# Output product in seven block products instead of eight, with more work for GpSimd and the DMA queue, in a fused retention and feed-forward kernel

## The chip, the cores and the metric

The kernel runs on one core of a Trainium2 chip. The metric is the device time of one launch in microseconds; a run is given by the median of its executions. The kernel before took 176.74 us (median of 3, 176.43 to 178.31).

## What is computed

A recurrent retention layer over 4 batches, 8 heads, 768 tokens and 64 dimensions per head feeds a multiplicative feed-forward layer with `d_model` 512 and `d_ff` 1024. All inputs and the output are float32.

```
for t in range(S):
    state = gamma[None, :, None, None] * state + einsum('bhd,bhe->bhde', k[:, :, t], v[:, :, t])
    y[:, :, t] = scale * einsum('bhd,bhde->bhe', q[:, :, t], state)
x = y.transpose(0, 2, 1, 3).reshape(3072, 512)
out = ((x @ w1) * (x @ w2) @ w3) @ w_out
```

## The kernel before, in words

The 3072 rows are cut into 12 steps of 256 tokens, three for each batch. A step `n` runs in chunk form: `scores(n)` makes key-query products, `mask` multiplies them by a 0/1 triangle on VectorE, `kv(n)` and `state(n, i)` carry the decayed state, `inter(n, ...)` and `av(n)` add up the layer's output in two PSUM banks, and `x_out(n, g)` multiplies it by a table of decays and writes it as fp16 tile `xt`, which is the feed-forward layer's input, already turned. Keys and queries are cast to fp16 by `cast`, values by `cast_v` (with a table of decays). The scores need keys and queries turned. For steps 0 to 4 TensorE does that (`turn`, then a copy out of PSUM by `turned`), for steps 5 to 11 a transposing DMA on SyncE's queue does it (`dma_turn`).

The two weights behind the product are folded once at the start: `w3_mm` makes `W3O = w3 @ w_out` (1024x512, eight tiles `w3o`), so that the feed-forward part of a step is `h = (x @ w1) * (x @ w2)` and `out = h @ W3O`. For steps 2 to 11 `h` is made with seven block products instead of eight, for each half `u` of `d_ff`: `sums` makes four sums of blocks of `xt` (tiles `sodd` and `seven`), `combine` has made the matching four sums of blocks of the weights once (tiles `wt`), `prod(n, u, i)` runs product `i` of 7 in eight 128x128 matmuls, `seed` copies one bank of partial sums to another, `keep_part` copies partial sums to SBUF (`u`, `p`), `c12` and `c22` add them, and `half_h` multiplies two results to a part of `h` (tile `ht`). The output product of a step is `o_unit(n, tb)` for its two blocks `tb` of 128 rows: 8 matmuls of 128x128 weights from `ht` against 512 columns of `w3o` (16 of 256 columns for a few steps), then `o_copy` scales it on ScalarE into `osb`.

Everything stands in an order written by hand: each engine runs its instructions in the order of the calls. Steps 0 to 2 are written call by call, steps 3 to 11 by a loop, in which step `n`'s feed-forward products follow step `n + 1`'s scores:

```
        o_unit(n - 1, 1, ("X1" if n < 11 else "S1",))
        o_copy(n - 1, 1)
        ...
        if n < 9:
            dma_turn("k", n + 3)
            if n < 8:
                load("v", n + 4)
        if 3 < n < 10:
            cast_v(n + 2, "g")
        if 3 < n < 9:
            cast("q", n + 3, "g")
            dma_turn("q", n + 3)
        quick(n, ("F1", "F0"), ("K", "F2"), ("X0", "X1"))
```

All loads, turns and stores are issued by SyncE into one queue; `"v"`, `"g"` and `"s"` name VectorE, GpSimd and ScalarE. Loads go to 18 staging buffers (`st`); a queue, key or value load of a step is 0.5 MB. All stores of finished rows come at the end of the program, behind the last load and turn.

Of the kernel before, what the change touches and what calls it, by code (L numbers as in the profile page):

```python
# [21 lines left out]
def kernel(  # L22
# [16 lines left out]
    NSTAGE = 18  # L39
# [138 lines left out]
    VN = const.tile([128, 2, H], FP, name="VN")  # L178
    YS = const.tile([128, 2, NP, 128], FP, name="YS")
# [10 lines left out]
    W3O = [wpool.tile([128, DM], HP, name=f"w3o_{i}") for i in range(8)]  # L190
# [11 lines left out]
    def tables():  # L202
        nc.scalar.activation(VS[:, :, :], vs_x[:, :, :], AF.Exp)
        for p in range(NP):
            nc.scalar.activation(YS[:, :, p, :], col_f[:, :, :], AF.Exp, scale=LGP[:, p : p + 1])
# [75 lines left out]
    def w3_out(f, eng):  # L281
        assert w3n[f] == 8
        copy(eng, W3O[f][:, :], acc.pop(f)[:, :])
# [86 lines left out]
    def scores(n, tags, hp=None):  # L370
# [10 lines left out]
        else:  # L381
            ps = [bank(t, [128, NP, 2, 64]) for t in tags]
            for a in range(NP):
                for s in range(2):
                    for r, g in QUARTERS:
                        nc.tensor.matmul(
                            ps[r][half(g), a, s, :], lhsT=kT[n][half(r), s, a, half(g)],
                            rhs=qchunk(n, r, a, s, g), start=True, stop=True,
# [144 lines left out]
    def x_out(n, g):  # L533
# [5 lines left out]
        if n < EO:  # L539
# [4 lines left out]
            )  # L544
        else:
# [73 lines left out]
    def o_unit(n, tb, tags, cuts=((0, 512),)):  # L619
        assert ht_n[n] == 4  # L620
        for (c0, c1), tag in zip(cuts, tags):
# [3 lines left out]
            for f in range(8):  # L625
                for x in range(parts):
                    nc.tensor.matmul(  # L627
                        ps[:, x * w : (x + 1) * w], lhsT=HT[n][:, tb, f, :], rhs=W3O[f][:, c0 + x * w : c0 + (x + 1) * w],
# [4 lines left out]
    def o_part(n, tb, x, tag):  # L633
# [4 lines left out]
        for f in range(4 * x, 4 * x + 4):  # L638
            nc.tensor.matmul(  # L639
                ps[:, :], lhsT=HT[n][:, tb, f, :], rhs=W3O[f][:, :], start=(f == 0), stop=(f == 7),  # L640
            )
# [15 lines left out]
    def o_copy(n, tb, c0=0, c1=512):  # L657
        nc.scalar.activation(o_tile(n, tb)[:, c0:c1], o_ps.pop((n, tb, c0, c1))[:, :], AF.Copy, scale=final_scale)  # L658
        o_n[n] = o_n.get(n, 0) + (c1 - c0)
        o_n[n, tb] = o_n.get((n, tb), 0) + (c1 - c0)  # L660

# [254 lines left out]
    w3_mm(3, 2)
    w3_mm(4, 1)
    w3_mm(3, 1)
    w3_mm(5, 1)
    turn("k", 0, "F1")  # L920
    w3_mm(6, 2)
    w3_mm(2, 1)
    turn_w3(7, "S1")
    turned_w3(7, "s")
    cast("q", 0, "g")
    cast_wo(3, "v")
    w3_mm(5, 3)
    w3_mm(4, 3)
    w3_mm(3, 3)
    w3_mm(1, 3)  # L930
    w3_mm(2, 3)
    turn("q", 0, "F1")
    w3_mm(6, 1)
    w3_mm(7, 2)
    w3_mm(3, 0)
    w3_out(5, "v")
    turned("k", 0, "v")
    turned("q", 0, "v")
    w3_out(1, "s")
    w3_out(4, "s")  # L940
    cast_v(0, "g")
    w3_out(2, "s")
    cast("q", 1, "s")
    scores(0, ("K", "F1"), 0)
    scores(0, ("S0", "S1"), 1)
    w3_mm(6, 3)
    w3_mm(7, 1)
    kv(0, ("F0", "K"))
    w3_mm(6, 0)
    w3_mm(7, 3)  # L950
    w3_mm(7, 0)
    w3_out(6, "s")
    cast_w3(0, "g")
    step_decays()
    w3_out(3, "v")
    mask(0, 0, 0)
    mask(0, 1, 0)
    state(0, 1)
    mask(0, 0, 1)
    w3_out(7, "s")  # L960
    state(0, 2)
    mask(0, 1, 1)
    inter(0, 0, ("F0", "X1"))
    turn("q", 1, "F1")
    turn_w3(0, "S0")
    fence(0)
    state(0, 3)
    turned_w3(0, "v")
    inter(0, 1)
    av(0)  # L970
# [60 lines left out]
    combine(1, 1)
    combine(3, 1)
    cast_v(2, "g")
    rows(W2, 0, 0, 0)
    rows(W2, 0, 1, 0)
    rows(W1, 1, 1, 1)
    rows(W1, 1, 0, 2)
    rows(W1, 1, 0, 0)
    rows(W2, 0, 0, 2)
    rows(W1, 1, 0, 3)  # L1040
    rows(W2, 0, 0, 3)
    rows(W1, 1, 0, 1)
    rows(W1, 1, 1, 0)
    rows(W1, 1, 1, 3)
    rows(W1, 1, 1, 2)
    rows(W2, 1, 0, 2)
    rows(W2, 0, 1, 3)
    cast_v(3, "g")
    rows_out("b", 0, 0, 1)
    rows_out("b", 0, 0, 0)  # L1050
    rows_out("a", 1, 0, 1, "v")
    rows_out("a", 1, 0, 0, "s")
    cast("q", 2, "s")
    rows_out("a", 1, 1, 0, "s")
    rows_out("a", 1, 1, 1, "v")
    rows_out("b", 0, 1, 1)
    cast("k", 2, "v")
    combine(1, 0)
    rows_out("b", 0, 1, 0)
    rows(W2, 1, 0, 1)  # L1060
    rows(W2, 1, 0, 3)
    rows(W2, 1, 0, 0)
    rows(W2, 1, 1, 2)
    rows(W2, 1, 1, 0)
    rows(W2, 1, 1, 3)
    rows(W2, 1, 1, 1)
    o_part(0, 1, 0, "F0")
    turn("q", 2, "S0")
    turn("k", 2, "F2")
    turned("k", 2, "s")  # L1070
    turned("q", 2, "s")
    o_part(0, 0, 0, "F1")
    o_part(0, 0, 1, "X0")
    o_part(0, 1, 1, "S1")
    o_copy(0, 0)
    o_copy(0, 1)
    cast("k", 3, "s")
    rows_out("b", 1, 0, 1)
    rows_out("b", 1, 1, 1)
    rows_out("b", 1, 0, 0)  # L1080
    combine(2, 1)
    rows_out("b", 1, 1, 0)
    combine(2, 0)
    combine(4, 0)
    combine(4, 1)
    scores(2, ("S1", "F2"), 0)
    scores(2, ("S0", "X0"), 1)
    kv(2, ("K", "X1"))
    mask(2, 1, 0)
    state(2, 1)  # L1090
    mask(2, 1, 1)
    mask(2, 0, 0)
    mask(2, 0, 1)
    o_unit(1, 0, ("F1",))
    turn("k", 3, "F0")
    inter(2, 0, ("X1", "X0"))
    fence(2)
    kv(3, ("K", "F2"))
    inter(2, 1)
    av(2)  # L1100
    o_copy(1, 0)
    turned("k", 3, "s")
    state(3, 1)
    cast("q", 3, "g")
    turn("q", 3, "S1")
    o_unit(1, 1, ("S0",))
    fetch("v4")
    fetch("k4")
    fetch("q6")
    fetch("k5")  # L1110
    fetch("v5")
    fetch("q5")
# [155 lines left out]
```

## Time and profile before

| | |
|---|---|
| time, median of 3 | 176.74 us |
| span of the profiled execution (first to last instruction) | 175.2 us |
| TensorE (PE) matmul busy | 167.0 us, 95% of the span |
| VectorE (DVE) busy | 123.8 us, 71% |
| ScalarE (ACT) busy | 88.4 us, 50% |
| GpSimd (POOL) busy | 95.0 us, 54% |
| packets of the DMA queue, share of 16 engines | 93.6% |
| granted TensorE clock | 1.000 |

The profiled execution's own time isn't listed apart. Its span is 175.2 us, and the median of the runs is 1.5 us longer; what is worked out for the span is carried over to the runs with that difference. The chain of waits that ended last lies 74% on PE, 11% on DMA and 9% on SyncE's issuing (SPq). The idle of POOL is the number to keep beside PE's load: it is the engine that gets most of the added work.

### The profile page before, as it was taken

What the parts mean: (1) busy time and instruction counts of PE and PEld (TensorE: products, weight loads), DVE (VectorE), ACT (ScalarE), POOL (GpSimd) and SP (SyncE); (2) the same over time, 40 slices, a digit from 0 to 9 for tenths busy, and PEclk for the clock granted to TensorE, in tenths of its full rate; (3) what the DMA queues carried; (4) which work ended last, traced back from release to release, by engine and by line L of the source; (5) the groups of instructions that cost most, each with busy time, mean ns of one, the idle gap of its engine ahead of it and who ended that gap; (6) DMA issues with size and microseconds to landing.
All of it is one profiled execution on the core that took longest, in us unless ns stands there. A gap on an engine that the chain in (4) does not pass through costs nothing.

```text
span 175.2 us, 7306 instructions
## 1 busy us (share of the span) xinstructions
PE 167.0 (95%) x3196; PEld 135.9 (78%) x3196; DVE 123.8 (71%) x230; ACT 88.4 (50%) x160; POOL 95.0 (54%) x124
## 2 busy tenths in 40 slices
PE   7769999999999998999999999999999999999993
PEld 2349987878877698498799986959999598695972
DVE  0454168989899758777968689686796868956370
ACT  2025986534426884182561835618357183471832
POOL 3872267866054826079584792957819366123150
PEclk9999999999999999999999999999999999999999
DMA  5999999999999989998999999999991354092563
GB/s 206 396 418 361 314 324 344 410 391 292 282 218 218 248 187 241 146 221 182 181 241 184 163 235 165 229 183 187 195 179 24 64 201 167 9 397 80 237 247 121
DMA packets 76160, 39.80 MB, mean 227 GB/s; under 512 B 53088, under 2 KB 71776, under 8 KB 76128
## 3 DMA queue, kind: packets, MB, share of 16 engines
q1 hardware_dynamic: 76128, 39.33, 93.6%
q8 instruction: 25, 0.41, 1.0%
q14 instruction: 7, 0.06, 0.1%
HBM read 29.36 MB, written 6.29 MB: 204 GB/s over the span
## 4 chain that ended last, share of the span: by engine, by line
PE 74%; DMA 11%; SPq 9%; POOL 2%; ACT 1%; issue 1%; ACTq 0%
PE psF L752 24%; PE psF L627 9%; PE psX L627 8%; PE psK L752 5%; PE psS L627 5%; DMA st<-in_v_dram 5%; PE psX L752 5%; SPq L98 5%; SPq L85 4%; DMA st<-in_q_dram 3%; PE psF L604 3%; DMA st<-in_moe_w_dram 3%; PE psX L499 2%; PE psS L604 2%; PE psF L639 2%; PE psX L525 2%
## 5 line engine op out<-in xcount | busy, mean ns | idle before, releaser
L752 PEld LDWEIGHTS <-wt 128*128 128x128 f16 x640 | 37.4, 98 | 0.0
L627 PEld LDWEIGHTS <-ht 128*128 128x128 f16 x224 | 20.8, 98 | 14.6
L65 POOL TENSOR_TENSOR c<-u,p 128x512 f32<-128x512 f32 x20 | 25.1, 1277 | 10.9 <-DVE ht L65 9.0
L752 PEld LDWEIGHTS <-w 128*128 128x128 f16 x480 | 28.9, 98 | 2.1 <-issue 0.3
L62 ACT COPY u<-psF 128x512 f32<-128x512 f32 x40 | 23.4, 591 | 7.4 <-PE psF L752 7.3
L65 POOL TENSOR_TENSOR seven<-xt,seven 128x256 f16<-128x256 f16 x9 | 6.0, 672 | 33.5 <-PE psF L752 26.3
L65 POOL TENSOR_TENSOR v<-st,VN 128x1024 f16<-128x1024 f32 x9 | 17.2, 1907 | 4.4 <-PE psX L377 4.4
L752 PE MATMUL psF<-sodd,wt 128*128 128x128 f16 x240 | 18.1, 219 | 0.0
L65 DVE TENSOR_TENSOR c<-psK,u 128x512 f32<-128x512 f32 x10 | 6.9, 691 | 15.4 <-PE psK L752 13.7
L627 PE MATMUL psF<-w3o,ht 128*128 128x256 f16 (+1 forms) x96 | 17.2, 327 | 0.0
L546 DVE TENSOR_TENSOR xt<-psX,YN 128x512 f16<-128x512 f32 x18 | 11.6, 686 | 6.2 <-PE psX L525 6.2
L65 DVE TENSOR_TENSOR ht<-psF,c 128x512 f16<-128x512 f32 x20 | 13.7, 687 | 2.5 <-POOL c L65 2.1
L658 ACT ACTIVATE osb<-psF 128x512 f32<-128x512 f32 x8 | 4.8, 597 | 20.9 <-PE psF L627 18.3
L627 PE MATMUL psX<-w3o,ht 128*128 128x512 f16 (+1 forms) x80 | 15.2, 336 | 0.0
L65 DVE TENSOR_TENSOR ht<-psX,c 128x512 f16<-128x512 f32 x19 | 13.1, 691 | 1.9
L62 POOL CAST k<-st 128x1024 f16<-128x1024 f32 x9 | 9.4, 1046 | 8.2 <-DMA st<-in_k_dram 8.2
L604 PEld LDWEIGHTS <-w 128*128 128x128 f16 x128 | 12.1, 98 | 2.2 <-POOL w L62 0.4
L276 PEld LDWEIGHTS <-w3t 128*128 128x128 f16 x128 | 12.0, 98 | 1.4
L752 PE MATMUL psX<-xt,w 128*128 128x128 f16 x152 | 11.6, 219 | 0.0
L403 DVE TENSOR_TENSOR am<-psS,keep 128x512 f16<-128x512 f32 x17 | 10.9, 681 | 0.0
L752 PE MATMUL psF<-xt,w 128*128 128x128 f16 x160 | 10.6, 219 | 0.0
L752 PE MATMUL psF<-seven,wt 128*128 128x128 f16 x160 | 10.6, 219 | 0.0
(151 smaller groups left out, 353.7 us busy)
## 6 DMA issues: line engine op xcount, KB each, us to landing
st<-in_moe_w_dram SPq DMA_DIRECT2D x16, 512.0 KB, 7.7
st<-in_q_dram SPq DMA_DIRECT2D x12, 512.0 KB, 6.6
st<-in_k_dram SPq DMA_DIRECT2D x18, 256.0 KB, 5.2
st<-in_v_dram SPq DMA_DIRECT2D x18, 256.0 KB, 4.9
out_dram<-osb SPq DMA_DIRECT2D x9, 512.0 KB, 4.9
st<-in_moe_w_out_dram SPq DMA_DIRECT2D x4, 512.0 KB, 7.7
st<-in_k_dram SPq DMA_DIRECT2D x3, 512.0 KB, 10.9
st<-in_v_dram SPq DMA_DIRECT2D x3, 512.0 KB, 8.0
```

The costliest lines, as they stand in the source:

```text
L62: {"v": nc.vector.tensor_copy, "g": nc.gpsimd.tensor_copy, "s": nc.scalar.copy}[eng](dst, src)
L65: (nc.vector if eng == "v" else nc.gpsimd).tensor_tensor(dst, a, b, op)
L85: via.dma_start(t[:, :].rearrange("p (h x) -> p h x", x=2 * D), src.rearrange("h (p t) d -> p h (t d)", t=2))
L98: nc.sync.dma_start(t[:, :], src[i * 128 : (i + 1) * 128, :])
L276: nc.tensor.matmul(acc[f][:, cols], lhsT=w3t[f][:, g * 128 : (g + 1) * 128], rhs=WO[i][:, r, cols], start=(first and (r, c) == (0, 0)), st ...
L403: nc.vector.tensor_tensor(t[:, :, :, :].rearrange("p a s i -> p (a s) i"), ps[:, :, :, :].rearrange("p a s i -> p (a s) i"), keep64[:, :]. ...
L499: nc.tensor.matmul(dst, lhsT=TS[n, c][half(r), a, :], rhs=rhs, start=((g, o) not in begun), stop=False, skip_group_check=True,)
L546: nc.vector.tensor_tensor(XT[n][:, :, :, :].rearrange("p t a (s x) -> p (a s) t x", s=2)[:, :, :, g * 32 : (g + 1) * 32], x[:, :, :].rearr ...
L604: nc.tensor.matmul(rows_ps[w, n, uh][j // 2][:, j % 2, :], lhsT=W[d][:, f * 128 : (f + 1) * 128], rhs=XT[n][:, :, d, :], start=(first and ...
L627: nc.tensor.matmul(ps[:, x * w : (x + 1) * w], lhsT=HT[n][:, tb, f, :], rhs=W3O[f][:, c0 + x * w : c0 + (x + 1) * w], start=(f == 0 and x ...
L658: nc.scalar.activation(o_tile(n, tb)[:, c0:c1], o_ps.pop((n, tb, c0, c1))[:, :], AF.Copy, scale=final_scale)
L752: nc.tensor.matmul(ps[:, j, :], lhsT=lhsT, rhs=rhs, start=(opens and j == 0 and c == 0), stop=(i in (2, 3, 4) and j == 3 and c == 1), skip ...
```

## The change

- The output product of steps 2 to 10 is made with seven products of blocks (128 rows, half of `d_ff`, 256 columns) instead of eight. `out_combine` makes four sums of blocks of `W3O` once (`ot`), `h_sum(n, i)` four sums of blocks of `ht` for each step (`hs`, 128x512 fp16 each), `oprod(n, i)` runs a product as four matmuls against 256 columns, and `oseed`, `okeep`, `o11`, `o21`, `o12`, `o22` put the partial sums together and scale them. Step 11 and steps 0 and 1 keep `o_unit` and `o_part`.
- For steps 6 to 11 the query cast multiplies by a table of decays (`QS`), and `x_out` is a plain copy on ScalarE, where it was a product on VectorE.
- Keys and queries of steps 3 and 4 are turned by `dma_turn`, not by TensorE.
- The whole program stands in a new order, call by call; there are 16 staging buffers instead of 18, and stores of finished rows stand between the loads.

```
-    NSTAGE = 18
+    NSTAGE = 16
+    PRE = 6
...
+    QS = const.tile([128, 2, H], FP, name="QS")
...
-        if nm == "q" or n < EO:
+        if nm == "q" and n >= PRE:
+            tt(
+                eng, t[:, :, :].rearrange("p t (h d) -> p h t d", d=D),
+                src[:, :].rearrange("p (h t d) -> p h t d", t=2, d=D),
+                QS[:, :, :].rearrange("p t h -> p h t").unsqueeze(3).broadcast_to((128, H, 2, D)), MULT,
+            )
+        elif nm == "q" or n < EO:
...
+        elif n >= PRE:
+            nc.scalar.copy(
+                XT[n][:, :, :, :].rearrange("p t a (s x) -> p (a s) t x", s=2)[:, :, :, g * 32 : (g + 1) * 32],
+                x[:, :, :].rearrange("p a (s t i) -> p (a s) t i", s=2, t=2),
+            )
...
+    def h_sum(n, i, eng="v"):
...
+        a, b, op = {
+            1: lambda: (h_of(n, 0, 0), h_of(n, 0, 1), ADD),
+            2: lambda: (HS[n, 1][:, :, :], h_of(n, 1, 0), SUB),
+            3: lambda: (h_of(n, 1, 0), h_of(n, 0, 0), SUB),
+            4: lambda: (h_of(n, 1, 1), HS[n, 2][:, :, :], SUB),
+        }[i]()
+        tt(eng, t[:, :, :], a, b, op)
...
+    def oprod(n, i, tag=None):
+
+        key = {1: "A", 6: "A", 7: "A", 4: "A", 5: "B", 3: "B", 2: "C"}[i]
+        if i in (1, 5):
+            OB[n, key] = bank(tag, [128, 256])
+        ps = OB[n, key]
+        lhs, rhs = {
+            1: lambda: (h_of(n, 1, 0), blocks(0, 0)),
+            2: lambda: (h_of(n, 1, 1), blocks(1, 0)),
+            3: lambda: (HS[n, 4], blocks(1, 1)),
+            4: lambda: (h_of(n, 0, 1), OT[4]),
+            5: lambda: (HS[n, 1], OT[1]),
+            6: lambda: (HS[n, 2], OT[2]),
+            7: lambda: (HS[n, 3], OT[3]),
+        }[i]()
+        for f in range(4):
+            nc.tensor.matmul(
+                ps[:, :], lhsT=lhs[:, f, :], rhs=rhs[:, f, :], start=(i in (1, 5) and f == 0),
+                stop=(i in (2, 3, 4) and f == 3), skip_group_check=True,
+            )
...
+    def o22(n, eng="g"):
+        tt(eng, o_tile(n, 0)[:, 256:512], ov.pop((n, "u3")), ov.pop((n, "p5")), ADD)
+        o_done(n, 0)
...
-    for n in range(3, 12):
-        inter(n, 0, ("X0", "X1"))
-        fence(n)
...
+    dma_turn('k', 11)
+    sums(9, 4, 'g')
+    state(10, 4)
+    prod(9, 0, 5, 'K')
+    o_store_all(4)
```

What the new order does is seen at two places. The first is SyncE's queue in its last third, in the kernel before; `kT<-k` and `qT<-q` are turns, `st` loads, `out_dram` stores of finished rows (`osw` 0.25 MB, `osb` 0.5 MB).

```order
L333 DMA_TRANSPOSE kT<-k_3061 128x8x128
L90 DMA st<-in_v_dram 128x8x64 x2
L333 DMA_TRANSPOSE qT<-q_3103 128x8x128
L333 DMA_TRANSPOSE kT<-k_3402 128x8x128
L333 DMA_TRANSPOSE qT<-q_3454 128x8x128
L669 DMA out_dram<-osb 128x1024 x9
L665 DMA out_dram<-osw 128x512 x4
```

There the turned keys of step 11 (`k_3402`) have no store ahead of them. The same stretch of the queue in the changed kernel, up to the turned keys of step 11 (`k_3856`):

```order
L343 DMA_TRANSPOSE kT<-k_3251 128x8x128
L343 DMA_TRANSPOSE qT<-q_3520 128x8x128
L780 DMA out_dram<-osw 128x512
L784 DMA out_dram<-osb 128x1024
L343 DMA_TRANSPOSE qT<-q_3589 128x8x128
L91 DMA st<-in_v_dram 128x8x64 x2
L784 DMA out_dram<-osb 128x1024 x3
L343 DMA_TRANSPOSE kT<-k_3856 128x8x128
```

The queries of step 11 are turned ahead of its keys now, and stores stand between the turns: counted over the whole queue, four `osw` and five `osb` ahead of the last turn.

The second place is GpSimd in a step of the loop, before; `c` are the sums of `c22`, `t` the decayed state, `v`, `q` and `k` casts.

```order
L62 CAST k_3061<-st 128x1024
L65 TENSOR_TENSOR seven<-xt,seven 128x256
L65 TENSOR_TENSOR v_3101<-st,VN 128x1024
L62 CAST q_3103<-st 128x8x2x64
L65 TENSOR_TENSOR c_3201<-u_3199,p_3147 128x512
L65 TENSOR_TENSOR c_3223<-u_3221,p_3175 128x512
```

And one step of GpSimd in the changed kernel, from one step's `c` to the next one's:

```order
L66 TENSOR_TENSOR hs<-hs,ht 128x512
L66 TENSOR_TENSOR sodd<-xt 128x256
L66 TENSOR_TENSOR q_3520<-st,QS 128x8x2x64
L66 TENSOR_TENSOR seven<-xt,sodd 128x256
L66 TENSOR_TENSOR hs<-ht,hs 128x512
L66 TENSOR_TENSOR t_3607<-s_3552,GS 128x256
L66 TENSOR_TENSOR v_3623<-st,VN 128x1024
L66 TENSOR_TENSOR c_3667<-u_3658,p_3575 128x512
L66 TENSOR_TENSOR c_3694<-u_3683,p_3601 128x512
```

Two sums of `ht` (`hs`) and one more sum of `xt` have moved to it, and its query cast has two inputs now.

More of the change, by code (lines that the diff above doesn't have):

```diff
@@ L932 @@
[L932 to L946, printed above, removed]
+    fetch('r1')
+    step_decays()
+    warm(8, 'X1')
+    fetch('r4')
+    identity()
+    fetch('r5')
+    fetch('r3')
+    fetch('wo0')
+    fetch('wo3')
+    cast_w3_half(1, 1, 's')
@@ L1051 @@
[L1051 to L1074, printed above, removed]
-    o_copy(0, 0)
[L1076 to L1088, printed above, removed]
+    combine(1, 1, 'g')
+    rows(W2, 0, 0, 3)
+    rows_out('b', 0, 1, 1)
@@ new lines @@
+    h_sum(2, 1, 'g')
+    prod(2, 1, 7)
+    x_out(3, 0)
+    fetch('q6')
+    oprod(2, 1, 'F1')
+    keep_part(2, 1, 'u3')
+    x_out(3, 1)
+    cast('k', 5, 's')
+    h_sum(2, 2, 'g')
+    prod(2, 1, 4)
+    c22(2, 1, 'v')
+    prod(3, 0, 1, 'X0')
+    oseed(2, 'X1')
+    dma_turn('k', 5)
+    scores(4, ('S0', 'S1'))
+    h_sum(2, 3, 'g')
+    half_h(2, 1, 1)
+    oprod(2, 6)
+    mask(4, 1)
+    oprod(2, 5, 'F0')
+    okeep(2, 'u2')
+    sums(3, 1, 'g')
+    oprod(2, 2)
+    mask(4, 0)
+    seed(3, 0, 'S1')
@@ new lines @@
+    oprod(2, 7)
+    h_sum(2, 4, 'g')
+    okeep(2, 'p5')
+    sums(3, 3)
+    prod(3, 1, 1, 'S0')
+    o11(2)
+    sums(3, 2)
+    state(4, 1)
+    prod(3, 0, 2)
+    seed(3, 1, 'X1')
+    state(4, 2)
+    prod(3, 0, 6)
+    okeep(2, 'u3')
+    state(4, 3)
+    prod(3, 1, 6)
+    cast('q', 5, 's')
+    sums(3, 4)
+    o22(2)
+    state(4, 4)
+    prod(3, 0, 5, 'K')
+    out_combine(4)
+    prod(3, 1, 5, 'F2')
+    state(4, 5)
+    keep_part(3, 0, 'p5')
+    dma_turn('q', 5)
+    oprod(2, 3)
+    keep_part(3, 0, 'u2', 'v')
@@ new lines @@
+    prod(3, 1, 4)
+    fence(4)
+    h_sum(3, 1)
+    inter(4, 1)
+    av(4)
+    half_h(3, 1, 1)
+    h_sum(3, 2, 'g')
+    oprod(3, 1, 'X0')
+    x_out(4, 1)
+    kv(5, ('K', 'S1'), (1,))
+    scores(5, ('F2', 'X1'))
+    load('q', 7)
+    x_out(4, 0)
+    oprod(3, 5, 'S0')
+    oseed(3, 'F0')
+    h_sum(3, 4, 'g')
+    oprod(3, 2)
+    state(5, 1)
+    mask(5, 0)
+    prod(4, 0, 1, 'F1')
+    o11(3)
+    sums(4, 1, 'g')
+    oprod(3, 6)
+    okeep(3, 'p5')
+    sums(4, 3)
+    state(5, 2)
+    prod(4, 1, 1, 'F2')
@@ new lines @@
+    kv(6, ('K', 'X1'), (1,))
+    fence(5)
+    h_sum(4, 2, 'g')
+    inter(5, 1)
+    half_h(4, 1, 1)
+    av(5)
+    scores(6, ('S1', 'F0'))
+    x_out(5, 1)
+    oprod(4, 1, 'F1')
+    h_sum(4, 3, 'g')
+    oprod(4, 5, 'F2')
+    x_out(5, 0)
+    oseed(4, 'S0')
+    oprod(4, 6)
+    state(6, 1)
+    mask(6, 1)
+    h_sum(4, 4, 'g')
+    oprod(4, 2)
+    okeep(4, 'u2')
+    prod(5, 0, 1, 'X0')
+    okeep(4, 'p5')
+    mask(6, 0)
+    o11(4)
+    oprod(4, 7)
+    seed(5, 0, 'F0')
+    cast('q', 7, 'g')
@@ new lines @@
+    half_h(5, 0, 1)
+    fence(6)
+    h_sum(5, 1, 'g')
+    o_store(0, 1)
+    inter(6, 1)
+    av(6)
+    half_h(5, 1, 1)
+    kv(7, ('K', 'F0'), (1,))
+    scores(7, ('X1', 'S0'))
+    x_out(6, 0)
+    oprod(5, 1, 'X0')
+    cast('q', 8, 'g')
+    mask(7, 0)
+    x_out(6, 1)
+    oprod(5, 5, 'S1')
+    oseed(5, 'F2')
+    h_sum(5, 2)
+    prod(6, 1, 1, 'X1')
+    mask(7, 1)
+    prod(6, 0, 1, 'F1')
+    sums(6, 3)
+    oprod(5, 2)
+    state(7, 1)
+    sums(6, 1, 'g')
+    seed(6, 0, 'S0')
+    dma_turn('q', 8)
@@ new lines @@
+    prod(6, 1, 5, 'F0')
+    okeep(5, 'u3')
+    load('k', 10)
+    prod(6, 0, 3)
+    keep_part(6, 0, 'u3')
+    o22(5)
+    oprod(5, 3)
+    keep_part(6, 1, 'p5')
+    c12(6, 0)
+    prod(6, 1, 7)
+    c22(6, 0)
+    oprod(5, 4)
+    half_h(6, 0, 0)
+    prod(6, 1, 3)
+    o21(5)
+    o12(5)
+    prod(6, 1, 2)
+    keep_part(6, 1, 'u3')
+    c12(6, 1)
+    inter(7, 0, ('X0', 'S1'))
+    c22(6, 1)
+    load('q', 10)
+    prod(6, 0, 4)
+    fence(7)
+    half_h(6, 1, 0)
+    inter(7, 1)
+    av(7)
@@ new lines @@
+    half_h(6, 0, 1)
+    kv(8, ('K', 'S0'), (0,))
+    scores(8, ('F0', 'F2'))
+    h_sum(6, 1, 'g')
+    x_out(7, 1)
+    kv(8, ('K', 'S0'), (1,))
+    prod(6, 1, 4)
+    mask(8, 0)
+    x_out(7, 0)
+    oprod(6, 1, 'F1')
+    state(8, 1)
+    cast('k', 9, 'g')
+    prod(7, 0, 1, 'X0')
+    half_h(6, 1, 1)
+    oseed(6, 'S1')
+    prod(7, 1, 1, 'F0')
+    sums(7, 3)
+    h_sum(6, 2, 'g')
+    sums(7, 1)
+    oprod(6, 5, 'X1')
+    dma_turn('k', 9)
+    state(8, 2)
+    oprod(6, 2)
+    mask(8, 1)
@@ new lines @@
+    keep_part(7, 1, 'p5', 'v')
+    keep_part(7, 1, 'u2')
+    o_store(1, 0)
+    cast('k', 10, 'g')
+    oprod(6, 4)
+    c12(7, 0)
+    prod(7, 1, 3)
+    o12(6)
+    prod(7, 0, 7)
+    o22(6)
+    c12(7, 1)
+    prod(7, 0, 2)
+    load('v', 10)
+    keep_part(7, 0, 'u3')
+    prod(7, 1, 7)
+    half_h(7, 0, 0)
+    o21(6)
+    c22(7, 0)
+    prod(7, 1, 2)
+    keep_part(7, 1, 'u3')
+    inter(8, 0, ('F1', 'X1'))
+    half_h(7, 1, 0)
+    prod(7, 0, 4)
+    fence(8)
+    c22(7, 1)
+    o_store_all(3)
@@ new lines @@
+    inter(8, 1)
+    h_sum(7, 1)
+    av(8)
+    scores(9, ('S0', 'S1'))
+    half_h(7, 0, 1)
+    x_out(8, 1)
+    kv(9, ('K', 'F2'), (0,))
+    kv(9, ('K', 'F2'), (1,))
+    mask(9, 0)
+    prod(7, 1, 4)
+    x_out(8, 0)
+    h_sum(7, 2, 'g')
+    oprod(7, 1, 'X0')
+    state(9, 1)
+    prod(8, 1, 1, 'S0')
+    dma_turn('k', 10)
+    half_h(7, 1, 1)
+    oseed(7, 'X1')
+    sums(8, 1, 'g')
+    prod(8, 0, 1, 'F1')
+    mask(9, 1)
+    oprod(7, 6)
+    cast('q', 10, 'g')
+    sums(8, 3)
+    oprod(7, 2)
@@ new lines @@
+    half_h(8, 0, 1)
+    inter(9, 0, ('X0', 'F0'))
+    scores(10, ('F2', 'X1'))
+    h_sum(8, 1)
+    fence(9)
+    kv(10, ('K', 'S1'), (0,))
+    kv(10, ('K', 'S1'), (1,))
+    h_sum(8, 3)
+    inter(9, 1)
+    av(9)
+    h_sum(8, 2, 'g')
+    half_h(8, 1, 1)
+    oprod(8, 1, 'F1')
+    x_out(9, 1)
+    mask(10, 0)
+    oprod(8, 5, 'S0')
+    oseed(8, 'F0')
+    cast('k', 11, 'g')
+    x_out(9, 0)
+    oprod(8, 6)
+    mask(10, 1)
+    oprod(8, 2)
+    o22(7, 'v')
+    okeep(8, 'u2')
+    sums(9, 3, 'g')
@@ new lines @@
+    prod(9, 0, 4)
+    h_sum(9, 1)
+    inter(10, 0, ('F1', 'S0'))
+    half_h(9, 0, 1)
+    scores(11, ('S1', 'F0'))
+    fence(10)
+    kv(11, ('K', 'X1'), (0,))
+    kv(11, ('K', 'X1'), (1,))
+    inter(10, 1)
+    half_h(9, 1, 1)
+    av(10)
+    oprod(9, 1, 'X0')
+    x_out(10, 1)
+    state(11, 1)
+    oprod(9, 5, 'F2')
+    h_sum(9, 3)
+    oseed(9, 'S0')
+    x_out(10, 0)
+    h_sum(9, 2)
+    oprod(9, 2)
+    state(11, 2)
+    okeep(9, 'p5')
+    oprod(9, 6)
+    sums(10, 1)
+    h_sum(9, 4)
```

1050 lines of the change are left out of this document (732 added, 318 removed).

## The prediction

> **What bounds the kernel now.** I read the busy times of the engines first, then the chain of waits over the steps, then the DMA queue. The windows by stage (engine, busy us, number of instructions; at the end granted clock, DMA share, GB/s) show PE full and POOL half empty over the steps of the loop:
>
> ```profile
> 66.00:145.00 79.00, 78.20 (x1802) 66.90 (x1800) 61.38 (x120) 40.13 (x79) 51.02 (x46) 1.00 1.06 180
> 62.00:72.00 10.00, 8.98 (x241) 8.02 (x239) 6.46 (x12) 5.24 (x10) 4.22 (x4) 1.00 1.15 197
> ```
>
> The columns are PE, PEld, DVE, ACT, POOL: in 79 us PE lacks 0.8 us, POOL has 28 us to spare. The only visible hole of PE is at 62 to 72 us, 1.0 us. The chain of waits (start, length, what) shows where that hole comes from and what a step is made of:
>
> ```profile
> 62.95 6.12 DMA st<-in_q_dram
> 69.10 1.04 ACT q L62
> ...
> 72.77 1.73 PE psX L627 x8
> ...
> 86.48 0.45 PE psK L752 x8
> 86.93 1.34 PE psF L752 x24
> ...
> 94.92 1.75 PE psX L627 x16
> ...
> 97.56 0.45 PE psK L752 x8
> ```
>
> The hole is ScalarE's query cast, which waited for its load. From then on the chain is PE without a gap: the same product starts at 86.48 and 97.56, so a step takes 11.08 us, and PE's instruction stream is the bound. A matmul of 512 columns takes 1.73/8 = 0.216 us there, one of 256 columns 1.75/16 = 0.109 us, one of 128 columns 1.34/24 = 0.056 us. Ten columns cost the same in each form, so the time goes with the columns.
>
> **What PE loses.** A step's output product was 16 matmuls of 512 columns, 16 x 0.216 = 3.46 us (32 of 256 columns, 3.50 us, in steps 4 and 7). It is now 7 x 4 = 28 matmuls of 256 columns, 28 x 0.109 = 3.06 us: 0.40 us less in each of nine steps, 3.7 us. The four turns that leave PE are eight transposes each, with this row of the chain for one:
>
> ```profile
> 50.59 0.45 PE psS L341 x8
> ```
>
> That is 4 x 0.45 = 1.8 us. PE's stream gets 5.5 us shorter. The profiled execution has a span of 175.2 us, the median of the runs is 176.74 us, 1.5 us outside the span; with PE alone as the bound the time would be 176.7 - 5.5 = 171.2 us, and 170.2 us if the hole at 62 to 72 us went too. That is the lower end.
>
> **What POOL gains.** The groups of instructions of POOL, and one of DVE (count | busy us, mean ns | idle before):
>
> ```profile
> L65 POOL TENSOR_TENSOR c<-u,p 128x512 f32<-128x512 f32 x20 | 25.1, 1277 | 10.9 <-DVE ht L65 9.0 <-ACT u L62 1.9
> L65 POOL TENSOR_TENSOR v<-st,VN 128x1024 f16<-128x1024 f32 x9 | 17.2, 1907 | 4.4 <-PE psX L377 4.4
> L62 POOL CAST k<-st 128x1024 f16<-128x1024 f32 x9 | 9.4, 1046 | 8.2 <-DMA st<-in_k_dram 8.2
> L65 POOL TENSOR_TENSOR seven<-xt,seven 128x256 f16<-128x256 f16 x9 | 6.0, 672 | 33.5 <-PE psF L752 26.3 <-DVE seven L65 7.2
> L65 POOL TENSOR_TENSOR t<-s,GS 128x256 f16<-128x256 f32 x8 | 5.8, 731 | 0.1
> ...
> L65 DVE TENSOR_TENSOR sodd<-xt 128x256 f16<-128x256 f16 x20 | 5.6, 290 | 0.0
> ```
>
> From step 2's last sum `c` to step 9's, seven steps, POOL's list in the changed kernel holds 13 `c` (1.28 us each, 16.6), 19 sums `hs` of 128x512 fp16, 6 value casts (11.4), 4 query casts with two inputs (I take the value cast's 1.91, 7.6), 4 key casts (4.2), 9 sums of `xt` (6.0), 6 sums of 256 columns in `o22` and 5 `t` (0.73 each, 8.0). No row shows `hs`. It is bounded by 0.67 us (half its columns, same type) and 1.28 us (its columns, wider type); since 0.67 us for 256 columns is already the rate of 1.28 us for 512, I take 1.28: 24.3 us. The sum is 78.1 us. PE's seven steps are 7 x 10.64 = 74.5 us (11.08 less 0.44, since the step at 86.48 has the 256-column form). So POOL is short by 3.6 us even if it never waits. With the lower bound for `hs` the sum is 66.5 us and the price nothing.
>
> What is late then: `c` and `hs` stand behind casts in POOL's order, `half_h` on DVE waits for `c`, and PE's `oprod` waits for both. The price falls on PE.
>
> The Trainium skill (GPSIMD Engine Reference, Engine selection) says that VectorE should have elementwise work on two inputs, and that GpSimd takes about twice as long for it. The rows above give 672 against 290 ns, 2.3 times, for one shape. By that rule 19 sums belong on DVE, where the sum here would be without the term of POOL.
>
> VectorE gives up 12 `x_out` and the scalar engine takes them. Over the loop ACT's 40 of 79 us leave room for these and for the six short copies of a step, so I cost them at nothing; if ACT's cover failed, `fence` and `seed` would be late next, and PE behind them.
>
> **What the DMA queue gains.** Timeline of the queue's issues (start, length), and windows:
>
> ```profile
> 83.26 2.19 SPq L333 DMA_TRANSPOSE qT<-q  x1
> ...
> 93.33 3.26 SPq L333 DMA_TRANSPOSE qT<-q  x1
> 96.63 1.21 SPq L90 DMA_DIRECT2D st<-in_k_dram  x2
> ...
> 129.13 1.25 SPq L333 DMA_TRANSPOSE kT<-k  x1
> ```
>
> ```profile
> 0.00:39.00 39.00, 35.01 (x493) 26.24 (x494) 21.62 (x40) 19.17 (x32) 22.82 (x61) 1.00 1.01 352
> 40.00:50.00 10.00, 10.00 (x91) 8.49 (x89) 9.26 (x15) 3.49 (x5) 4.12 (x4) 1.00 1.13 273
> 50.00:60.00 10.00, 9.94 (x197) 7.02 (x196) 8.84 (x16) 6.40 (x9) 5.65 (x5) 1.00 1.07 226
> 96.50:97.50 1.00, 1.00 (x20) 0.99 (x18) 0.94 (x4) 0.79 (x2) 0.00 (x0) 1.00 0.08 18
> 153.00:158.00 5.00, 5.00 (x103) 4.90 (x102) 3.12 (x6) 3.55 (x7) 1.52 (x2) 1.00 0.98 385
> ```
>
> By 39 us the queue has moved 13.7 MB, which is all 26 weight and first loads. Up to 130.4 us it then issues almost without a gap. Around a turn it stands nearly still: the turn's issue lasts to 96.59, the next load starts at 96.63, and 96.5 to 97.5 moves 18 GB/s. So a turn costs the queue more than its 0.26 MB. Its price: from 83.26 to 130.38 lie ten turns, 4 query loads (0.52 MB at 273 GB/s, 1.9 us) and 8 key or value loads (at 226, 2.3 us), so (47.1 - 26.2)/10 = 2.1 us if the queue never stood. The least is its bytes at 226 GB/s, 1.2 us. I take 1.8, nearer to the tally, which holds some standing.
>
> The last turned keys before PE's last `scores` are due by this row of the tile `kT`:
>
> ```profile
> L386 PE MATMUL psS<-qT,kT x272: 186/194/213, 60.7 to 147.4; 64*64 64x64 f16 x136
> ```
>
> At 147.4 less the 1.8 and eight times 0.40 us that PE saves until then, they are due at 142.4. After 39 us the changed queue has ahead of them 12 loads of 1.9 and 18 of 2.3 us (64.2), 3.7 MB of stores at 385 GB/s (9.5), and all 18 turns, where it had 13 turns and no store by then. At 1.8 us a turn that ends at 39 + 64.2 + 9.5 + 32.4 = 145.1, 2.7 us late, and with a microsecond to landing 3.7. At 2.1 us it is 9 us late, at 1.2 us early by 7. Each step's casts, which stand in the orders of POOL, ACT and DVE, are late with it.
>
> The Trainium skill (DMA: Bandwidth & Descriptors, Latency and other measured facts) gives 261 GB/s as the effective rate of a transposing DMA. An estimate from that page is 1.0 us for 0.26 MB, at which the queue would be early and its term zero. The still microsecond above speaks against it.
>
> **The sum.** POOL's 3.6 us and the queue's 3.7 us are waits over the same steps and run side by side, so the larger counts: 171.2 + 3.7 = 174.9 us. The tail behind step 11's last product is the same code as before. In the opening the same 26 loads stand first in the queue, and two staging buffers less cost nothing while the queue is behind its consumers anyway. POOL gets seven sums of 128x1024 weights there, at most 4 x 0.67 = 2.7 us each, 19 us; between 40 and 60 us it has 10.2 us free (4.12 and 5.65 busy in the windows above). The bounds are nothing and 8.7 us; since step 2's products use these sums last of all, at about 62 us, I take nothing and leave the rest to the range.
>
> **Rivals.**
> (1) All is hidden: PE stays the bound, 171.2 us or 170.2. For it: POOL's 28 spare microseconds and `hs` unmeasured. Against it: the sum of 78 us for seven steps.
> (2) The queue becomes the bound, slower than before: at 2.1 us a turn, 171.2 + 9.1 = 180.3 us. The place is the turned keys and queries of steps 9 to 11, behind stores and turns. It decides from about 1.9 us a turn (5.5 us late), where the saving is gone. For it: the tally without idle, and the still microsecond. Against it: standing time in the tally, and loads above 226 GB/s around the turns.
> (3) VectorE holds the end: with step 9, 10 and 11's sums it has 8 `hs`, 16 `c` and `ht` of 0.69 us, and about 24 others, some 25 us beside PE's last 24. With its waits that adds 1 to 3 us to the forecast, 177.0 us. Against it: little of it stands in line at the very end.
>
> **How the numbers follow.** The forecast (POOL and queue give most of it back) gets 0.42, with its own range 173.0 to 177.5. (1) gets 0.24, (2) 0.22, (3) 0.12. A measurement of this kernel tells about 1% from no change, 175.0 to 178.5 us being within it. Of the forecast I count 0.17 as faster and 0.25 as within, (1) as faster, (2) as slower, (3) as 0.08 within and 0.04 slower: faster 0.41, within 0.33, slower 0.26. The range goes from 170.8, between the two ends of (1), to 180.3, the price of (2).
>
> **What would show it.** Right: PE busy near 161 us, with holes of its own ahead of `oprod` of the summed parts, ended by POOL; POOL over 90% busy from 67 to 145 us; `hs` near 1.28 us; a step near 11 us. The queue's step is right if a turn still has its still microsecond and the last `scores` start 3 to 4 us behind 142. It is wrong if steps take 10.6 us (then 1), if PE's longest waits are for DMA and casts, or for turned keys (then 2), or if DVE is full from 145 us on (then 3). A mean of `hs` below 1.0 us would take the main term away.

## The result: 13.5% slower

| | before | changed |
|---|---|---|
| time, median of 4 | 176.75 us (176.43 to 178.31) | 201.29 us (199.91 to 202.24) |
| span of the profiled execution | 175.2 us | 199.9 us |
| ratio, 95% interval | | 1.135 (1.128 to 1.143) |

The forecast was 174.9 us, and its range ended at 180.3. Some executions of a kernel run a few per cent longer at a lower granted clock, whatever was changed; the ratios below compare the others alone, so they can differ from a quotient of medians, and the traces of the two runs with idle instructions and of the shorter list are of such longer executions.

The page of the changed kernel: busy times, the granted clock in 40 slices, the share of the DMA queue, and the engines in the chain of waits.

```profile
PE 171.9 (86%) x3240; PEld 145.7 (73%) x3240; DVE 161.9 (81%) x265; ACT 100.8 (50%) x203; POOL 127.0 (64%) x137
...
PEclk9999999999999699999699699999999999999999
...
q1 hardware_dynamic: 80352, 40.38, 80.7%
...
PE 47%; DVE 28%; DMA 8%; issue 6%; ACT 3%; SPq 3%; POOL 3%; DVEq 0%; POOLq 0%; ACTq 0%
```

PE is no longer full, and VectorE, which had no row in the chain before, now has 28% of it. GpSimd has 3%, and the queue was busier before (93.6%). The same stretch of 79 us as in the prediction, by windows (PE, PEld, DVE, ACT, POOL, clock, DMA share, GB/s):

```profile
66.00:145.00 79.00, 67.29 (x1436) 60.35 (x1436) 72.44 (x114) 38.46 (x83) 56.00 (x48) 0.94 0.88 174
170.00:180.00 10.00, 9.86 (x248) 8.73 (x247) 9.69 (x23) 5.42 (x15) 1.70 (x2) 1.00 0.11 43
```

PE lacks 11.7 us, where it lacked 0.8; DVE is at 92%, GpSimd at 71%. At 170 to 180 us, where GpSimd has almost nothing left to do, PE is full again, though DVE is still busy for 9.7 of 10 us. Why VectorE is so busy stands in its groups of instructions (count | busy us, mean ns | idle before):

```profile
L66 DVE TENSOR_TENSOR sodd<-xt 128x256 f16<-128x256 f16 x14 | 11.7, 841 | 0.0
L66 DVE TENSOR_TENSOR hs<-ht 128x512 f16<-128x512 f16 x11 | 9.6, 888 | 0.0
...
L66 DVE TENSOR_TENSOR t<-psK,t 128x256 f16<-128x256 f32 x16 | 6.6, 413 | 0.1
L66 DVE TENSOR_TENSOR seven<-xt,sodd 128x256 f16<-128x256 f16 x8 | 6.1, 768 | 0.3 <-POOL sodd L66 0.2
```

`sodd` took 290 ns before and takes 841 now, the same instruction with the same shape. `t`, with one input in PSUM, keeps its 0.41 us. The undisturbed length of an `hs` on VectorE is 0.41 us (at 173 us, with GpSimd idle). The timeline of VectorE and GpSimd shows what the long ones wait for (start, length):

```profile
61.08 2.58 POOL L66 TENSOR_TENSOR wt<-w,w 128x1024 f16<-128x1024 f16 x1
...
61.60 2.21 DVE L66 TENSOR_TENSOR sodd<-xt 128x256 f16<-128x256 f16 x1
...
63.62 1.95 POOL L66 TENSOR_TENSOR v<-st,VN 128x1024 f16<-128x1024 f32 x1
63.73 2.38 DVE L66 TENSOR_TENSOR wt<-w,wt 128x1024 f16<-128x1024 f16 x1
66.04 0.28 DVE L66 TENSOR_TENSOR seven<-xt,sodd 128x256 f16<-128x256 f16 x1
...
66.37 0.93 PE L867 MATMUL psF<-seven,wt 128*128 128x128 f16 x7 [3.38 <-DVE seven L66]
```

`sodd` begins at 61.60, in the middle of GpSimd's sum, and ends at 63.81, 0.15 us after that ends at 63.66. The next sum, `wt`, begins at 63.73, meets the value cast, and ends 0.54 us after that ends at 65.57. With GpSimd free, `seven` takes 0.28 us. PE waited 3.38 us for these. In this trace a sum of two fp16 tiles stands still until GpSimd's running instruction is over. That holds for all of them: of VectorE's 47 sums `sodd`, `seven` and `hs`, 26 began inside an instruction of GpSimd, and each ended 0.14 to 0.15 us (256 columns) or 0.28 to 0.29 us (512 columns) after it; in the kernel before it was one of 31. A cast on GpSimd, which has one input, holds a sum too (first pair). The third and fourth line show a cast on VectorE, undisturbed 0.69 us, behind a sum of GpSimd, and the last two that it works the other way as well: GpSimd's `v`, 1.9 us elsewhere, waits for VectorE's `q`.

```profile
108.53 1.10 POOL L63 CAST k<-st 128x1024 f16<-128x1024 f32 x1
108.65 1.12 DVE L66 TENSOR_TENSOR sodd<-xt 128x256 f16<-128x256 f16 x1
...
38.80 2.44 POOL L66 TENSOR_TENSOR ot<-w3o 128x1024 f16<-128x1024 f16 x1
39.75 2.04 DVE L63 CAST w<-st 64x1024 f16<-64x1024 f32 x1
...
153.12 1.75 DVE L66 TENSOR_TENSOR q<-st,QS 128x1024 f16<-128x1024 f32 x1
153.75 2.88 POOL L66 TENSOR_TENSOR v<-st,VN 128x1024 f16<-128x1024 f32 x1
```

### The profile page after: what moved, and what is told of

Its sections match the earlier page's. It is cut to its first block, busy times and chain, and to the rows that moved or that the text cites. A ratio compares the mean times of both kernels' runs of the same rounds, so it can differ in the third digit from the quotient of the medians.

```text
span 199.9 us, 7480 instructions
## 1 busy us (share of the span) xinstructions
PE 171.9 (86%) x3240; PEld 145.7 (73%) x3240; DVE 161.9 (81%) x265; ACT 100.8 (50%) x203; POOL 127.0 (64%) x137
## 4 chain that ended last, share of the span: by engine, by line
PE 47%; DVE 28%; DMA 8%; issue 6%; ACT 3%; SPq 3%; POOL 3%; DVEq 0%; POOLq 0%; ACTq 0%
DMA st<-in_moe_w_dram 8%; PE psF L867 8%; PE psX L867 6%; PE psS L867 5%; DVE sodd L66 4%; PE psK L867 4%; DVE ht L66 4%; PE psF L736 3%; DVE hs L66 3%; DVE t L66 3%; PE psF L619 3%; PE psX L736 3%; DVE seven L66 3%; DVE am L413 3%; SPq L104 2%
## 5 line engine op out<-in xcount | busy, mean ns | idle before, releaser
L66 POOL TENSOR_TENSOR c<-u,p 128x512 f32<-128x512 f32 x14 | 17.8, 1281 | 14.6 <-ACT u L63 14.5
L736 PEld LDWEIGHTS <-hs 128*128 128x128 f16 x144 | 12.7, 98 | 5.6 <-DVE hs L66 2.0
L63 ACT COPY u<-psF 128x512 f32<-128x512 f32 x16 | 9.3, 589 | 10.4 <-PE psF L867 10.4
L66 DVE TENSOR_TENSOR sodd<-xt 128x256 f16<-128x256 f16 x14 | 11.7, 841 | 0.0
L736 PEld LDWEIGHTS <-ht 128*128 128x128 f16 x108 | 9.7, 100 | 2.3 <-DVE ht L66 0.8
L746 ACT ACTIVATE osb<-psF 128x256 f32<-128x256 f32 x19 | 7.4, 388 | 6.1 <-PE psF L736 6.0
L66 DVE TENSOR_TENSOR hs<-ht 128x512 f16<-128x512 f16 x11 | 9.6, 888 | 0.0
L619 PE MATMUL psF<-xt,w 128*128 128x256 f16 x48 | 8.8, 273 | 0.8 <-issue 0.8
L280 PE MATMUL psF<-wo,w3t 128*128 128x256 f16 x64 | 9.0, 273 | 0.6 <-DVE wo L63 0.6
L867 PE MATMUL psF<-sodd,wt 128*128 128x128 f16 x112 | 9.5, 236 | 0.0
```

Of the source, the lines that this page charges most:

```text
L63: {"v": nc.vector.tensor_copy, "g": nc.gpsimd.tensor_copy, "s": nc.scalar.copy}[eng](dst, src)
L66: (nc.vector if eng == "v" else nc.gpsimd).tensor_tensor(dst, a, b, op)
L280: nc.tensor.matmul(acc[f][:, cols], lhsT=w3t[f][:, g * 128 : (g + 1) * 128], rhs=WO[i][:, r, cols], start=(first and (r, c) == (0, 0)), st ...
L619: nc.tensor.matmul(rows_ps[w, n, uh][j // 2][:, j % 2, :], lhsT=W[d][:, f * 128 : (f + 1) * 128], rhs=XT[n][:, :, d, :], start=(first and ...
L736: nc.tensor.matmul(ps[:, :], lhsT=lhs[:, f, :], rhs=rhs[:, f, :], start=(i in (1, 5) and f == 0), stop=(i in (2, 3, 4) and f == 3), skip_g ...
L746: nc.scalar.activation(dst, src, AF.Copy, scale=final_scale)
```

## The experiments

Theory 1: VectorE's sum of two tiles in SBUF is blocked by a running GpSimd instruction. Theory 2: VectorE and GpSimd have too much work, blocked or not. Theory 3: the new order and its DMA queue set the time. Ratios are to the kernel before on the same chip, with a 95% interval.

**Sums from GpSimd to VectorE**

```
-    h_sum(2, 1, 'g')
+    h_sum(2, 1)
-    sums(3, 1, 'g')
+    sums(3, 1)
...   (29 such lines)
```

> All 29 sums of the changed kernel that stand on GpSimd (19 of ht, 10 of xt) go to VectorE; nothing else changes. Theory 1 (a VectorE sum of two fp16 tiles in SBUF stands still until GpSimd's running instruction ends): GpSimd runs about 30 us less, so fewer sums meet it; mean of sodd, seven and hs falls from 0.77 to 0.89 us towards 0.5 us, time 188 to 195 us. Theory 2 (VectorE simply has too much work): 29 more instructions of 0.28 to 0.41 us, about 11 us more on an engine that is 81% busy, time 205 to 212 us. Theory 3 (the new order and its queue set the time, the sums don't): 199 to 203 us.

Measured: 195.1 us, ratio 1.094 (1.070 to 1.117). VectorE got 29 instructions more, and its busy time did not grow:

```profile
PE 169.4 (87%) x3240; PEld 141.8 (73%) x3240; DVE 160.8 (83%) x294; ACT 100.8 (52%) x203; POOL 97.3 (50%) x108
```

```profile
L66 DVE TENSOR_TENSOR sodd<-xt 128x256 f16<-128x256 f16 x20 | 7.9, 400 | 0.0
```

Theory 2's 205 us is out, and so is theory 3's 199. `sodd` fell to 400 ns, `hs` only to 529 to 713 ns, the time to the upper edge of theory 1's range.

**Eight block products again**

```
-    oprod(3, 5, 'S0')
...
-    oprod(3, 2)
+    o_unit(3, 0, ('S0',))
+    o_unit(3, 1, ('F0',))
...   (no h_sum, out_combine, oseed, okeep, o12, o22)
```

> The changed kernel with the output product of steps 2 to 10 in eight block products again (o_unit and o_copy at the places of the products); no sums hs, no ot, no o12, o22. The order, the turns of steps 3 and 4 and the decayed query casts stay. PE gets 3.7 us more. Theory 1: VectorE's 14 hs and GpSimd's 19 are gone, but query and value casts still stand against sodd and seven, which stay above 0.5 us; time 184 to 192 us. Theory 2 (work alone): VectorE loses 5.7 us of hs and 3.7 us of o12 at undisturbed durations, time 190 to 195 us, and sodd and seven stay as long as they are. Theory 3 (order and queue): 198 us or more.

Measured: 194.0 us, ratio 1.090 (1.069 to 1.111). The time lies in theory 2's range and 2 us above theory 1's, the durations speak against theory 2, which had them unchanged: `sodd` 387 ns, less than theory 1 had, `seven` 494 and 605 ns. So the sums of `ht` are not the whole loss; with them gone, GpSimd still meets the sums of `xt`. How the rest divides between the blocking, the longer list of GpSimd and the order, this run does not tell.

**Idle instructions on GpSimd, in the kernel before**

```
+        for _ in range(3):
+            tt("g", busy[:, 0:512], yn2[:, 0:512], yn2[:, 512:1024], ADD)
         sums(n, 3)
...   (the second run: nc.gpsimd.memset(busy[:, 0:1536], 0.0) in place of tt)
```

> The kernel before, with three idle sums of 128x512 on GpSimd in each step 3 to 11, read from the table YN and written to a tile that nobody reads, placed ahead of the sum seven in GpSimd's order, where it sat idle about 3 us. 27 instructions of about 1.2 us, 33 us in all. Theory 1: VectorE's sodd and seven wait for them, means from 0.29 to 0.6 us or more; time 179 to 186 us. Theory 2 (work alone): sodd and seven stay at 0.29 us, what GpSimd does later by itself costs 0 to 2 us, time 176.5 to 178.5 us.

> As the one with three idle sums, but with three memsets of 128x1536 fp16, which read nothing, in their place; about 1.3 us each, to be read from the trace. If the VectorE sum waits for GpSimd's reading (theory 1 in the narrow form), sodd and seven stay at 0.29 us and the time is the kernel before's plus 0 to 2 us. If it waits for any instruction of GpSimd (theory 1 in the wide form), it is as in the kernel with three idle sums. Theory 2: both kernels take the same time, and sodd and seven 0.29 us in both.

The groups of instructions, GpSimd's added one and VectorE's `sodd`, first with sums, then with memsets:

```profile
L65 POOL TENSOR_TENSOR busy<-YN 128x512 f16<-128x512 f32 x27 | 34.5, 1277 | 1.4
...
L65 DVE TENSOR_TENSOR sodd<-xt 128x256 f16<-128x256 f16 x20 | 13.1, 661 | 0.0
```

```profile
L1198 POOL MEMSET busy<- 128x1536 f16 x27 | 37.2, 1377 | 1.0
...
L65 DVE TENSOR_TENSOR sodd<-xt 128x256 f16<-128x256 f16 x20 | 5.6, 290 | 0.0
```

This is the cleanest pair. GpSimd is about as long occupied in both (129.7 and 132.0 us in all); only where the added instructions read does `sodd` go from 290 to 661 ns. It is theory 1 in the narrow form. The Trainium skill (SBUF — State Buffer, Who interferes with whom) states just that: a VectorE instruction with two SBUF inputs contends with a GpSimd instruction that reads SBUF, not with one that only writes it. The two runs agree. It calls the contention an exclusive lock, which the ends of the 26 sums above bear out. In time the pair is inconclusive: ratios 1.035 (0.999 to 1.072) and 1.022 (0.983 to 1.061).

**The changed kernel, GpSimd hardly reading**

```
     def tt(eng, dst, a, b, op):
+        if eng == "g":
+            nc.gpsimd.tensor_tensor(one(dst), one(a), one(b), op)
+            nc.gpsimd.memset(dst, 0.01)
+            nc.gpsimd.memset(dst, 0.01)
+            return
...   (copy: the same with one memset)
```

> The changed kernel in which GpSimd reads next to nothing: each of its sums and casts is one instruction on a few elements (which keeps the wait for its input), followed by one memset (cast) or two memsets (sum) of the whole output tile with a constant, by the durations seen for memsets (0.83 ns a column and 0.1 us) about as long as before: 0.74 us for 256 columns, 1.17 us for 512, 2.0 us for 1024, 1.07 us for a cast of 1024. So what GpSimd computes is left out; its order, waits and occupation stay, VectorE's instructions are all the same. Theory 1 (blocked sums): sodd and seven 0.29 us, hs 0.41 us, VectorE busy near 138 us, PE's holes mostly gone, time 174 to 183 us. Theory 2 (work alone): 196 to 202 us, since the work is the same. Theory 3 (the new order and its queue): 196 to 202 us too, with the sums at 0.3 to 0.4 us.

> The same edit on the kernel before (GpSimd's sums and casts left out in the same way): what the edit itself brings where VectorE's sums hardly meet GpSimd. All theories: 174.5 to 177.5 us. Theory 1: wt and the sums at their shortest, sodd 0.28 us.

Measured: 188.1 us, ratio 1.060 (1.053 to 1.068), and for the kernel before with the edit 181.3 us, 1.020 (1.015 to 1.026). In the changed kernel with the edit:

```profile
PE 167.9 (90%) x3240; PEld 141.9 (76%) x3240; DVE 136.1 (73%) x265; ACT 100.5 (54%) x203; POOL 133.5 (72%) x308
...
POOL 43%; PE 28%; DMA 16%; issue 4%; SPq 3%; DVE 2%; ACT 1%; POOLq 0%; ACTq 0%; DVEq 0%
```

```profile
L80 DVE TENSOR_TENSOR hs<-ht 128x512 f16<-128x512 f16 x11 | 4.4, 418 | 0.0
L80 DVE TENSOR_TENSOR sodd<-xt 128x256 f16<-128x256 f16 x14 | 3.9, 284 | 0.0
```

The same 265 instructions of VectorE take 136.1 in place of 161.9 us: 25.8 us of its busy time was standing still. (The same edit in the kernel before changes VectorE's busy time by 1.3 us, from 123.8 to 122.5.) The ratio falls by 0.075, 13 us, so theories 2 and 3 (196 to 202 us) are out as the main cause. But 174 to 183 us was missed too. VectorE has nearly left the chain (2%), and GpSimd's list is the bound now, at 43%. Part of that is the edit, whose imitation is longer than the original, 133.5 for 127.0 us. In the kernel before, too, it adds to GpSimd's list (102.8 for 95.0 us) and costs 2.0%, so the expected 174.5 to 177.5 us was missed there.

**GpSimd's list shorter, then nine turns fewer**

```
             nc.gpsimd.memset(dst, 0.01)
-            nc.gpsimd.memset(dst, 0.01)
```

```
     def dma_turn(nm, n, via=None):
+        if nm == "q":
+            return
-        dst[n] = t = new_T(nm)
+        dst[n] = qT[n] = t = new_T(nm)
```

> As the changed kernel without GpSimd's reads, but with one memset in place of two for each of its sums, so that GpSimd is also about 45 us less occupied (133 us before). It leaves out what GpSimd computes, as there. What is left of the loss is then the new order, ScalarE's share and the DMA queue. If the loss was VectorE's blocked sums and, behind them, the length of GpSimd's list: 171 to 177 us, PE over 95% busy from 60 us on, chain mostly PE. If the order or the queue (18 turns, stores between the loads) has a price of its own: 182 us or more, with PE waiting for turned keys or for copies.

> As the run with GpSimd's reads left out and one memset for each sum, and besides the nine turns of queries are left out: the scores take the turned keys in their place. The queue loses nine of its 18 turns, some 16 us at 1.8 us a turn. If the queue was what bound that run (chain 26% DMA, PE waiting for turned keys): PE is the bound, 170 to 174 us, which is the floor of 171.2 us that PE's shorter stream gives. If the new order itself has a price: 180 us or more, as in that run (182 to 183 us).

> The changed kernel with the nine turns of queries left out in the same way, and nothing else touched: GpSimd reads and blocks VectorE's sums as in the changed kernel. If the blocked sums set its pace and the queue only waits behind them: 196 to 202 us, next to nothing gained. If the queue set its pace: 185 us or less.

Measured: ratio 1.027 (1.018 to 1.036) with the short list, 0.986 (0.981 to 0.992) with nine turns fewer besides, but 1.121 (1.115 to 1.128), 200.4 us, for the changed kernel that only lost the nine turns. The chain of the short list, its queue, and PE's longest waits:

```profile
q1 hardware_dynamic: 80352, 40.38, 93.7%
...
PE 61%; DMA 26%; ACT 4%; SPq 3%; issue 2%; DVE 2%; POOL 1%; DVEq 0%; POOLq 0%
```

```profile
PE psX L409 <- DMA kT<-k: 3.1, 1, 3.1
PE psS L409 <- DMA kT<-k: 2.6, 3, 1.5
```

There PE's longest waits are for turned keys of the queue. The stretch of 79 us shows the three limits one behind the other; the rows are, in this order, nine turns fewer alone, GpSimd not reading, its list short as well, and nine turns fewer as well:

```profile
66.00:145.00 79.00, 66.37 (x1556) 59.33 (x1556) 74.06 (x116) 39.08 (x85) 57.55 (x48) 0.98 0.82 178
```

```profile
66.00:145.00 79.00, 69.99 (x1608) 63.38 (x1606) 63.34 (x124) 42.45 (x96) 71.25 (x165) 1.00 1.06 203
```

```profile
66.00:145.00 79.00, 72.07 (x1723) 66.30 (x1720) 65.33 (x128) 42.27 (x97) 44.60 (x116) 0.98 1.14 206
```

```profile
66.00:145.00 79.00, 77.74 (x1855) 72.19 (x1853) 69.59 (x140) 49.04 (x111) 50.12 (x132) 1.00 1.07 207
```

PE goes from 66.4 to 70.0, 72.1 and 77.7 of 79 us. Only the last is bound by PE. Taking turns away first changes little (1.121 for 1.135), since the queue waited behind the blocked sums. The steps of the ratio, in this order from 1.135: 0.075 (13 us) for the blocked sums, 0.033 (6 us) for the length of GpSimd's list, 0.041 (7 us) for the turns. In another order the shares may come out otherwise. The new order and the 16 staging buffers were not run alone; once the three are eased, no loss is left for them to explain.

**Parts of the change, in the kernel before**

Step 5's queries loaded first:

```
-    fetch("q6")
+    fetch("q5")
     fetch("k5")
     fetch("v5")
-    fetch("q5")
+    fetch("q6")
```

> The kernel before with one exchange in the queue: the queries of step 5 are loaded ahead of those of step 6, in the place at which the load of step 6 stood. Its only hole of PE over the steps (1.0 us at 62 to 72 us) was ended by ScalarE's cast that waited for this load. 175.7 us, 1.0 us faster, if nothing else waits there; 176.7 us if the chain goes on through the next load.

The same, with step 4's turns on the queue:

```
     cast("q", 4, "s")
+    dma_turn("k", 4)
+    dma_turn("q", 4)
+    fetch("q6")
...
-    turn("k", 4, "X1")
-    turned("k", 4, "v")
...
-    turn("q", 4, "S1")
...
-    turned("q", 4, "v")
```

> The kernel before with the queries of step 5 loaded first (as in the run on that alone), and keys and queries of step 4 turned by the queue, behind the loads of step 5, in place of PE. PE loses 16 transposes, 0.9 us, VectorE two copies of 0.69 us. No sum goes to GpSimd. By my prices 0.9 us from PE and the 0.8 us of the exchange: 175.0 us, ratio 0.990. If a turn at this place makes the loads behind it late (queries of step 6, keys of step 6): 177 us or more.

Decayed queries alone, with the lines of the diff for `PRE`, `QS`, `cast` and `x_out`:

> The kernel before with one part of the change alone: query casts of steps 6 to 11 multiply by the table of decays (GpSimd, 1.95 us in place of 1.05), x_out of these steps is a plain copy on ScalarE (0.59 us) in place of a product on VectorE (0.69 us). Theory 1: GpSimd runs 5.4 us more, at places where few sums stand; 176 to 178 us. Theory 2: the same. Theory 3 doesn't touch it. It is not the cause if it stays under 178 us.

Step 5's queries first: 176.3 us, ratio 0.992 (0.988 to 0.997), about the microsecond that was expected. Of the versions that compute the whole result it is the one that beats both kernels. With step 4's turns besides: ratio 1.033 (1.024 to 1.041), 182.6 us for a kernel before of 176.75, where 0.990 was expected. PE now waits for the turned queries:

```profile
PE psS L386 <- DMA qT<-q: 2.7, 1, 2.7
```

What these turns save PE (0.9 us) is less than what they make late. The decayed queries alone: ratio 1.005 (1.001 to 1.009), by the same scale 177.6 us, within the 178 us that were set; they are not the cause.

## Why the prediction was wrong

- **The step that failed** is that VectorE stands in the sum with no term. Of VectorE the prediction says only that it "gives up 12 `x_out`", and rival (3) gives it 1 to 3 us at the end; the waits over the steps are POOL's and the queue's alone, as if VectorE's durations, 290 ns for `sodd`, held whatever GpSimd does. That row was taken where GpSimd was idle: the prediction's own row of `seven` on GpSimd shows 33.5 us of idle ahead of its nine, and only one of VectorE's 31 sums began inside a GpSimd instruction. The change fills these gaps, `sodd` goes to 841 ns, and of the 38.1 us by which VectorE's busy time grew 25.8 are standing still. Without GpSimd's reads 13 of the 24.5 us are gone. No rival had this.
- **The path** was wrong with it. The forecast had PE's holes ahead of `oprod`, ended by POOL; the largest one shown stands ahead of `prod` and is ended by VectorE's `seven`, and the chain has 28% of VectorE and 3% of POOL.
- **The sums of weights on GpSimd**, also costed at nothing, take part in the hole of 3.38 us at 63 to 66 us: `wt`, 2.6 us, held `sodd`, and the value cast behind it held VectorE's own `wt`.
- **GpSimd's sum** was near for `hs` (1.17 to 1.22 us for 1.28) and low for the casts of values (2.15 for 1.91), some of which wait for VectorE, and it was wrong as the bound: GpSimd is 71% busy between 66 and 145 us, not over 90%. It becomes the bound when the blocking is gone (71.3 of 79 us, 90%), with about 6 us for 3.6, the imitation and a list cut by 45 us included.
- **The queue's term** (3.7 us) stood behind the others. Where it could be seen, nine of 18 turns were worth 7 us. Rival (2) had the mechanism; in the changed kernel the nine turns are worth little (1.121, 1.115 to 1.128, against 1.135, 1.128 to 1.143). The term's microsecond to landing came from no row and is too short: in the kernel before turned keys landed 6.6 us after their issue began, and the issue takes 2.8 of them (medians).
- **Side by side, the larger counts** was the right form, as the turns that were taken away first show; but the largest limit was missing from the list.
- **PE's saving** of 5.5 us is shown in part: with all three limits eased the kernel is 1.4%, about 2.4 us, faster than before. PE is busy for 165.2 us there, 1.8 less than before, and not near 161. The other 3 us to the floor of 171.2 us stay open. The turns' part of it costs more than it saves when it is made alone: two of the four turns gave 1.033, where the run without them gave 0.992.
- **Rival (3)** named the right engine at the wrong place: VectorE held the steps between 66 and 145 us. At 170 to 180 us, near the end, it was nearly full too (9.7 of 10 us), but PE was as well (9.9).
- The rule on elementwise work that the prediction cited would put the 19 sums on VectorE. The run that did so, with ten sums of `xt` besides, took 195 us: `hs` is held there by GpSimd's casts and by its `c`.

## What to carry to other kernels

A duration is good only for what the neighbouring engine did meanwhile: before moving work onto an idle engine, look at whose short instructions run in its gaps. Two-input sums of SBUF tiles on VectorE and reading work on GpSimd exclude each other in these traces, and so did casts of SBUF tiles from fp32 to fp16 on VectorE; so count them as one engine, or let one input come from PSUM, as in `t`. Where several limits lie close together, ease them one after the other, since removing the second one first shows next to nothing.

## What was not expected of the hardware

A blocked sum counts as busy, so nothing in the busy shares or in the waits names GpSimd; the mean against an undisturbed row does, and the common end in the timeline. And some of PE's holes cost more than their length. Windows of the changed kernel:

```profile
106.40:110.10 3.70, 1.97 (x24) 1.45 (x23) 3.70 (x6) 2.02 (x5) 3.70 (x4) 1.00 0.08 16
110.10:112.60 2.50, 2.44 (x25) 2.44 (x25) 2.10 (x6) 0.59 (x1) 2.50 (x3) 0.55 0.99 190
```

After 3.7 us in which PE was busy for 1.97, the granted clock was 0.55. It was 0.51 and 0.52 after two more such holes (PE busy for 0.49 of 3.4 us from 62.5, and 0.72 of 3.4 from 93.2), but 1.00 after 136 to 140 us, in which PE was busy for 1.92; what decides, these runs don't tell. Nor is it the main price: over 66 to 145 us the mean granted clock was 0.94, an estimate of at most 79 x 0.06 = 4.7 us. The chain has eight matmuls of 128 columns there that took 0.85 us, where eight took 0.45 in the kernel before:

```profile
107.12 1.60 DVE seven L66
108.73 1.04 DVE sodd L66
109.77 0.34 DVE t L66
110.11 0.04 issue
110.16 0.85 PE psK L867 x8
```
